# How far ahead of the first row stores a fused attention and routing kernel loads: three steps instead of seven, with four row buffers

## The chip, the core and the metric

The kernel runs on one core of one Trainium2 chip. The metric is the device time of one execution in microseconds (us). The core has a matrix engine (PE in the profile, with its weight loads as PEld), a vector engine (DVE), a scalar engine (ACT), a general engine (POOL) and a sync engine (SP), which here only issues DMAs; SPq is its queue in the trace. PEclk is the clock that the matrix engine was granted, as a share of full speed.

## What is computed

The reference runs a linear attention with decay over q, k and v of shape (4, 8, 768, 64), reshapes its result to 3072 rows of 512, and sends each row through one of eight feed-forward experts, chosen by the largest gate logit:

```python
for b in range(nb):                                   # blocks of 64 positions
    intra = einsum('bhic,bhjc->bhij', qb, kb) * Dmask
    intra = einsum('bhij,bhjd->bhid', intra, vb)
    inter = einsum('bhid,bhde->bhie', qb * lam_pow, kv_state)
    out[:, :, sl] = intra + inter
    kv_state = lam_block * kv_state + einsum('bhsd,bhse->bhde', kb * rev_pow, vb)
x = out.transpose(0, 2, 1, 3).reshape(B * S, H * D)   # 3072 x 512
logits = x @ w_gate
expert_idx = argmax(logits, axis=1)                   # and gate_w, its softmax weight
for e in range(8):
    out[mask] = gate_w[mask, None] * (maximum(xe @ w1[e], 0.0) @ w2[e])
```

All is in float32.

## The kernel before

**Two parts.** The first part, up to about 187 us of the trace, is the attention. It uses blocks of 128 positions, so there are six of them, and takes two of the four batches at a time: twelve steps, 0 to 11, in the order (block 0, batches 0 and 1), (block 0, batches 2 and 3), (block 1, batches 0 and 1) and so on. Every step leaves two row tiles x of 128 x 512, which are stored to a table `xs` in device memory. The second part gathers the rows of each expert from that table and runs the eight feed-forward passes. The lists that say which row goes to which expert (`slots`) are filled by POOL during the attention, by indirect DMAs (`put`, L422).

**One step, as the matrix engine runs it.** The loop at L832 overlaps three steps. In its turn i the engine first multiplies the attention output of step i-1 by a permutation with the gate's columns beside it (`leave`, then `rows`, L345 and L347, PSUM tiles `tx`), then transposes q and k of step i+1 (`turn_q` L234, `turn_k` L249), then does step i itself: q against the running state (L291), the state's growth `cp` (L320), scores against v (L303), q against the state once more (L291); and at the end the scores q k of step i+1 (L267). I call one turn of this loop a step. ACT copies each `tx` out of PSUM: the logits at L351, the row tile x at L353. DVE adds the grown state at L337, for which POOL has scaled the old one (L335). PE, DVE, ACT and SP run in exactly the order in which the code issues their work (`manual_schedule`, L114 and L823). An instruction that waits holds up everything behind it on its engine.

**Loads.** `load(i)` (L94) fetches q, k and v of a step with three DMAs of 512 KB, all on the SP queue (for step 0 they are halves, and k goes by the ACT queue). At L114 the loads of steps 0 to 6 are issued, before anything else on SP. From turn 3 on, each turn issues one more load, that of step i+4 (L835); it comes right behind the row stores of that turn. Loads 0, 1, 7 and 2, 3, 8 use buffers of the expert weights (`IN_WEIGHTS`), and the others use a pool of three.

**Row stores.** `store_rows` (L357) stores the two row tiles of step i-1 in turn i, with two DMAs of 256 KB on the SP queue. The row tiles rotate through three buffers (L341, tag `x`), so the copy at L353 into a fourth tile waits until the store of the first has landed. The feed-forward passes use the same tag for rows that they read back (L700).

**What else stands near.** `zeros` is a tile of 128 x 128 with a place of its own. DVE reads it once, in turn 0, for the decay tables (L773), and POOL stores a row of it to `xs` at the beginning (L780). In turn 8 the weights of the first pass are loaded (L837, 4 MB), in turn 10 the list of that pass, `list_0a` (L840, L458), and in turn 11 its rows are gathered and brought into blocks (`xg`, `xe`, `xb`). PE's first feed-forward products are L533.

Of the kernel before, what the change touches and what calls it, by code (L numbers as in the profile page):

```python
# [10 lines left out]
F32 = mybir.dt.float32  # L11
# [10 lines left out]
def kernel(  # L22
# [29 lines left out]
    nc = tc.nc  # L52
    B, H, S, D = q.shape
    N, MD = out.shape
    E = moe_w_gate.shape[1]
    F = moe_w1.shape[2]
    P = 128
# [19 lines left out]
    const = ctx.enter_context(tc.tile_pool(name="const", bufs=1))  # L77
# [10 lines left out]
    order = [(n, b) for n in range(NSTEP) for b in range(0, B, 2)]  # L88
    loaded = {}
    IN_WEIGHTS = {0: "w1", 1: "w1", 2: "w2", 3: "w2", 7: "w1", 8: "w2"}  # L90
    AT_ONCE = 7
    lam_bc = const.tile([P, H], F32, name="lam_bc")

    def load(i):  # L94

        n, b0 = order[i]
        shp = [P, 2, H, D]
        if i in IN_WEIGHTS:
            whole = wpool.tile([P, 3] + shp[1:], F32, tag=IN_WEIGHTS[i], name="qkv_in")
            loaded[i] = [whole[:, j] for j in range(3)]  # L100
        else:
            loaded[i] = [qkv.tile(shp, F32, tag=name, name=f"{name}_in") for name in "qkv"]
        per = 2 if i else 1
        for t, src in zip(loaded[i], (q, k, v)):
            queue = nc.scalar if i == 0 and src is k else nc.sync
            for b in range(0, 2, per):
                queue.dma_start(
                    out=t[:, b:b + per].rearrange("p b h d -> p (b h) d"),
                    in_=src[b0 + b:b0 + b + per, :, n * C:(n + 1) * C, :].rearrange(
                        "b h s d -> s (b h) d"))  # L110
            if i == 0 and src is q:
                nc.sync.dma_start(out=lam_bc, in_=lam.partition_broadcast(P))

    with tc.manual_schedule(engines={mybir.EngineType.SP}):  # L114
        for i in range(AT_ONCE):
            load(i)
# [16 lines left out]
    make_upper_triangular(nc, before, val=1.0, diag=False)  # L133
    ones = const.tile([P, P], BF16, name="ones")
    nc.vector.memset(ones, 1.0)
    zeros = const.tile([P, P], F32, name="zeros")
    nc.vector.memset(zeros, 0.0)

    rev = const.tile([P, E], F32, name="rev")
    nc.gpsimd.iota(rev, pattern=[[-1, E]], base=E, channel_multiplier=0,  # L140
# [56 lines left out]
    def load_weights(e, pin=lambda inst: inst):  # L197
        return load_first(e, pin), load_second(e, pin)
# [4 lines left out]
    work = ctx.enter_context(tc.tile_pool(name="work", bufs=2))  # L203
# [5 lines left out]
    def bank(i, shape, name):  # L209
        return ps.tile(shape, F32, tag=f"bank{i}", name=name)  # L210


    st = once.tile([P, B, HP, D], F32, tag="h2", name="st")
    halves = [slice(0, D), slice(D, P)]

    def pin(inst):
        return tc.keep_in_program_order(inst)
# [9 lines left out]
    def turn_q(m, s):  # L229
        shp = turned_shape  # L230
        tq = bank(2 * s, shp, "tq")
        for i, b in itertools.product(range(HP // 2), range(2)):
            h = s * HP + 2 * i
            nc.tensor.transpose(tq[:, i, b, :], m.q[:, b, h:h + 2, :], ident)  # L234
        qT = work.tile(shp, F32, tag="qT", name="qT")
        nc.scalar.copy(qT, tq)
        m.qT.append(qT)
        if m.n > 0:
            qsT = work.tile(shp, F32, tag="qsT", name="qsT", bufs=4)
            nc.vector.tensor_mul(  # L240
                qsT, tq, qdec[:, s * HP // 2:(s + 1) * HP // 2].unsqueeze(2).to_broadcast(shp))
            m.qsT.append(qsT)

    def turn_k(m, s):
        shp = turned_shape
        tk = bank(2 * s + 1, shp, "tk")
        for i, b in itertools.product(range(HP // 2), range(2)):
            h = s * HP + 2 * i
            nc.tensor.transpose(tk[:, i, b, :], m.k[:, b, h:h + 2, :], ident)  # L249
        kT = work.tile(shp, F32, tag="kT", name="kT")  # L250
        nc.scalar.copy(kT, tk)
        m.kT.append(kT)
        if m.n < NSTEP - 1:
            shp = [P, 2, HP, D]
            kd = work.tile(shp, F32, tag="kd", name="kd")
            hs = slice(s * HP, (s + 1) * HP)
            pin(nc.gpsimd.tensor_tensor(out=kd, in0=m.k[:, :, hs],  # L257
                                        in1=kdec[:, hs].unsqueeze(1).unsqueeze(3).to_broadcast(shp),
                                        op=ALU.mult))
            m.kd.append(kd)  # L260
# [77 lines left out]

    def rows(m, b, lg):

        x = work.tile([P, MD], F32, tag="x", name="x", bufs=3)  # L341
        tx = [bank(4 + 2 * b + c, [P, 2, W], f"tx{c}") for c in range(DC // 2)]
        for c, t in enumerate(tx):
            flat = t.rearrange("p j w -> p (j w)")
            nc.tensor.matmul(flat[:, :W], lhsT=m.xT[b][:, 2 * c, :], rhs=back[:, c, :W],  # L345
                                 start=True, stop=False, skip_group_check=True)
            nc.tensor.matmul(flat[:, P:P + W], lhsT=m.xT[b][:, 2 * c + 1, :],  # L347
                                 rhs=back[:, c, W:], start=False, stop=True,
                                 skip_group_check=True)
        for c, t in enumerate(tx):  # L350
            nc.scalar.copy(lg[:, c, :], t[:, 0, P:])  # L351

            nc.scalar.copy(x.rearrange("p (a d f) -> p d a f", a=P // Q, d=DC)[:, 2 * c:2 * c + 2],  # L353
                           t[:, :, :P].rearrange("p d (a f) -> p d a f", f=Q))
        m.x.append(x)
# [101 lines left out]
    def load_list(m):  # L457
        nc.sync.dma_start(out=m.list[:, :len(m.takes), :], in_=m.rows)  # L458
# [238 lines left out]
    def take_rows(m, ts):  # L697
        for t in ts:
            w = m.widths[t]
            m.y.append(work.tile([P, MD], F32, tag="x", name="y", bufs=3))  # L700
            pin(nc.sync.dma_start(out=m.y[t][:w], in_=m.ye[Q + t * P:Q + t * P + w, :]))

    def give_rows(m):
# [85 lines left out]
    def begin(i):  # L789
        n, b = order[i]  # L790
        m = SimpleNamespace(n=n, b=b, qT=[], qsT=[], kT=[], kd=[], mt=[], xT=[], x=[])
        m.q, m.k, m.v = loaded[i]
        return m
# [3 lines left out]
    def leave(m):  # L797
        for b in range(2):
            n, bs = group_of[m.n, m.b + b]
            i = bs.index(m.b + b)  # L800
            if i == 0:
                lgs[0] = small.tile([P, len(bs), DC // 2, E], F32, tag="lg", name="lg")
            rows(m, b, lgs[0][:, i])
        store_rows(m)
        if i == len(bs) - 1:
            chosen.append(choose(n, bs, lgs[0]))
            return chosen[-1]
# [15 lines left out]
    with tc.manual_schedule(engines={mybir.EngineType.PE, mybir.EngineType.DVE,  # L823
                                     mybir.EngineType.Activation, mybir.EngineType.SP}):
        cur, last = begin(0), None
        for s in range(2):
            turn_q(cur, s)
        for s in range(2):
            turn_k(cur, s)
        for s in range(2):  # L830
            score(cur, s)
        for i in range(len(order)):  # L832
            due = chosen.pop() if chosen else None
            new = leave(last) if last else None
            if i >= 3 and i + 4 < len(order):  # L835
                load(i + 4)
            if i == len(order) - 4:  # L837
                weights.append(load_weights(0))
            if i == len(order) - 2:
                load_list(passes[0])  # L840
            if i == len(order) - 1:
                for t in range(TE):
                    keep(passes[0], t)
                take_blocks(passes[0])
            ahead = begin(i + 1) if i + 1 < len(order) else None
            if ahead:
                for s in range(2):
                    turn_q(ahead, s)
                    turn_k(ahead, s)
            if i == 0:  # L850
                later_decays()
            if new:
                weigh(*new)
            if due:
                put(*due)
                if due[:2] == early:
                    start_early()
            attend_states(cur, 0)
            grow(cur)
            attend(cur)  # L860
            attend_states(cur, 1)
            to_sbuf(cur)
            update(cur)
            if i == len(order) - 2:
                for t in range(TE):
                    take(passes[0], t, 1 + (NSTEP - 2) * B * C)
            if ahead:
                for s in range(2):
                    score(ahead, s)
            last, cur = cur, ahead  # L870
        put(*chosen.pop())
        turn(passes[0])
        weigh(*leave(last))
        put(*chosen.pop())
# [95 lines left out]
    with tc.If(most > 0):  # L970
        for i in range(E):
            tiles = nc.values_load(beyond[0:1, i:i + 1], min_val=0, max_val=MORE)
            with tc.If(tiles > 0):
# [4 lines left out]
                with tc.For_i(0, tiles, 1) as r:  # L978
                    m = sized(P, 1)
# [36 lines left out]
```

## Time and profile before

| what | value |
|---|---|
| median of three timed runs | 511.45 us (508.19, 511.45, 511.73) |
| the profiled execution's own time | 507.75 us |
| its span, first to last instruction | 506.0 us |
| around the span | 1.75 us |
| PE busy | 438.6 us (87%) |
| DVE, POOL, ACT busy | 255.9, 253.8, 121.8 us |
| mean granted PE clock | 0.939 |
| DMA | 96.77 MB, mean 191 GB/s |

The profile's lines are read as follows. A group or a wait names the engine, the operation, the tiles as output<-input, and the line of the kernel as L341. A row of the timeline gives the start and the length in us, and in brackets how long the engine was idle before it and what ended that wait. A row of the stretches ("from:to length, ...") gives each engine's busy time with its instruction count, then PEclk, the busy share of the DMA engines (above 1 where packets overlap) and GB/s. A row of the waits gives the total, how many times, and the longest.

### The profile page before, as it was taken

The numbers are of one execution on the slowest core, as the hardware profiler recorded it, in microseconds if no ns is written. First come the engines' busy times: TensorE is split into PE (matmuls) and PEld (weight loads), VectorE is DVE, ScalarE is ACT, GpSimd is POOL, SyncE is SP. The second block draws the span as 40 slices with busy tenths as digits, with TensorE's granted clock in tenths as the row PEclk, the third lists the DMA queues.
The fourth block names the chain that finished last, engine by engine and source line by source line (L and its number), as shares of the span: only waits on it lengthen the run. The fifth ranks groups of instructions, "written<-read, shape, count | busy, mean of one in ns | idle before, by whom it ended". The sixth has DMA issues, their size and how long they took to land.

```text
span 506.0 us, 9177 instructions
## 1 busy us (share of the span) xinstructions
PE 438.6 (87%) x3559; PEld 409.1 (81%) x3559; DVE 255.9 (51%) x519; ACT 121.8 (24%) x300; POOL 253.8 (50%) x194
## 2 busy tenths in 40 slices
PE   4870596969698929999999999999999889999994
PEld 4760586959597718489999999999999889999963
DVE  3530245445255623105795592983593883594431
ACT  2420243424253310010310230231230120230410
POOL 6210232432523333268987559938279946279201
PEclk9995597979799969999999999999999989999998
DMA  9999574949592431896988967784989492963301
GB/s 180 237 221 218 141 156 98 200 95 197 116 339 81 148 84 28 241 341 198 290 276 215 367 196 243 206 278 116 307 277 263 124 316 98 281 215 82 119 18 48
DMA packets 131763, 96.77 MB, mean 191 GB/s; under 512 B 83600, under 2 KB 107412, under 8 KB 131711
## 3 DMA queue, kind: packets, MB, share of 16 engines
q1 hardware_dynamic: 124287, 82.16, 60.2%
q0 software_dynamic: 5344, 13.41, 8.8%
q10 hardware_dynamic: 2080, 0.52, 0.6%
q8 instruction: 30, 0.49, 0.4%
q14 instruction: 22, 0.18, 0.1%
HBM read 70.96 MB, written 25.20 MB: 190 GB/s over the span
## 4 chain that ended last, share of the span: by engine, by line
PE 48%; DVE 5%; SPq 3%; issue 3%; DMA 2%; POOL 1%; POOLq 0%; DVEq 0%
PE p L658 22%; PE p L634 22%; PE p L722 2%; DMA xb<-xe 1%; PE po L750 1%; DVE hT L618 1%; SPq L458 1%; SPq L481 1%; DMA xg<-xs,list 1%; SPq L495 1%; DVE yb L691 1%; DVE s_h L616 1%; DVE s_h L617 1%; DVE hT L642 0%; DVE xgT L525 0%
## 5 line engine op out<-in xcount | busy, mean ns | idle before, releaser
L504 POOL DMA_INDIRECT out_dram<-o,list x24 | 24.4, 1018 | 60.8 <-ACT o L710 39.5
L643 ACT ACTIVATE hT<-hT 128x408 f32<-128x408 f32 (+4 forms) x56 | 29.4, 527 | 100.9 <-DVE hT L642 96.7
L658 PE MATMUL p<-hT,w2t 128*128 128x204 f32 (+3 forms) x288 | 50.9, 330 | 0.0
L422 POOL DMA_INDIRECT slots<-entry,slot_i x24 | 23.5, 977 | 50.4 <-DVE slot_i L420 29.4
L658 PEld LDWEIGHTS p<-hT,w2t 128*128 128x128 f32 x288 | 48.3, 190 | 0.0
L634 PE MATMUL p<-xgT,w1t 128*128 128x204 f32 (+4 forms) x224 | 41.7, 328 | 0.7 <-DVE t_sd L564 0.7
L257 POOL TENSOR_TENSOR kd<-qkv_in,kdec 128x512 f32<-128x512 f32 x12 | 12.3, 1041 | 52.2 <-PE cp L320 40.4
L634 PEld LDWEIGHTS p<-xgT,w1t 128*128 128x128 f32 x224 | 37.4, 190 | 1.0 <-issue 1.0
L345 PE MATMUL tx<-back,xT 128*128 128x136 f32 x96 | 23.5, 332 | 15.4 <-DVE st L337 14.7
L273 DVE TENSOR_TENSOR mt<-sp,decay 128x512 f32<-128x512 f32 x48 | 29.9, 682 | 7.9 <-PE sp L267 7.5
L291 PE MATMUL op<-qsT,st 64*64 64x128 f32 x320 | 14.5, 290 | 21.7 <-ACT x L353 21.6
L642 DVE TENSOR_TENSOR hT<-p,u_qsT 128x408 f32<-128x408 f32 (+4 forms) x42 | 23.5, 559 | 17.7 <-PE p L634 16.5
L533 PE MATMUL ph<-xgT,w1t 128*128 128x256 f32 (+1 forms) x128 | 24.1, 350 | 8.9 <-DVE lg_sum L366 8.9
L345 PEld LDWEIGHTS tx<-back,xT 128*128 128x128 f32 x96 | 17.5, 225 | 17.0 <-issue 14.9
L574 POOL TENSOR_TENSOR s_k<-w1t 128x1024 f32<-128x1024 f32 x7 | 16.6, 2365 | 28.3 <-DMA w1t<-in_moe_w_dram 28.2
L533 PEld LDWEIGHTS ph<-xgT,w1t 128*128 128x128 f32 x128 | 20.7, 201 | 11.7 <-DVE lg_sum L366 9.1
L291 PEld LDWEIGHTS op<-qsT,st 64*64 64x64 f32 x320 | 9.3, 136 | 24.8 <-ACT x L353 22.2
L525 DVE STREAM_TRANSPOSE xgT<-xb 128x768 f32<-128x768 f32 (+3 forms) x16 | 16.5, 1029 | 25.2 <-DMA xb<-xe 24.8
L498 POOL DMA_INDIRECT xg<-xs,list x24 | 24.1, 1002 | 8.9 <-issue 5.4
L545 ACT COPY u_qT<-p 128x408 f32<-128x408 f32 (+5 forms) x21 | 10.0, 476 | 74.0 <-PE p L634 45.5
L267 PE MATMUL sp<-qT,kT 64*128 64x128 f32 x384 | 26.2, 280 | 1.1 <-issue 0.9
L337 DVE TENSOR_TENSOR st<-cp,sd 128x512 f32<-128x512 f32 x8 | 5.5, 692 | 42.1 <-POOL sd L335 33.4
(182 smaller groups left out, 1043.5 us busy)
## 6 DMA issues: line engine op xcount, KB each, us to landing
w1t<-in_moe_w_dram SPq DMA_DIRECT2D x8, 2048.0 KB
w2t<-in_moe_w_dram SPq DMA_DIRECT2D x8, 2048.0 KB
xs<-x SPq DMA_DIRECT2D x24, 256.0 KB
xe<-xg SPq DMA_DIRECT2D x21, 256.0 KB
y<-ye SPq DMA_DIRECT2D x17, 256.0 KB
q_in<-in_q_dram SPq DMA_DIRECT2D x6, 512.0 KB
k_in<-in_k_dram SPq DMA_DIRECT2D x6, 512.0 KB
v_in<-in_v_dram SPq DMA_DIRECT2D x6, 512.0 KB
```

The lines of the kernel that those rows point to most:

```text
L267: nc.tensor.matmul(sp[u][:, i, b, :], lhsT=m.kT[s][halves[u], i, b, :], rhs=m.qT[s][halves[u], i, b, :], start=(i == 0 and b == 0), stop=( ...
L273: nc.vector.tensor_mul(mt[:, u], sp[u], decay[:, u, s * HP // 2:(s + 1) * HP // 2].unsqueeze(2).to_broadcast(shp))
L291: nc.tensor.matmul(out_at(m, b, u, hp), lhsT=st[halves[u], m.b + b, hp, :], rhs=m.qsT[hp // 2][halves[u], hp % 2, b, :], start=(way == 0 a ...
L345: nc.tensor.matmul(flat[:, :W], lhsT=m.xT[b][:, 2 * c, :], rhs=back[:, c, :W], start=True, stop=False, skip_group_check=True)
L422: put = pin(nc.gpsimd.indirect_dma_start(out=slots, out_offset=bass.IndirectOffsetOnAxis(ap=slot_i[:, i:i + 1], axis=0), in_=entry[:, n, b ...
L498: return nc.gpsimd.indirect_dma_start(out=dst, out_offset=None, in_=xs[:rows, :], in_offset=bass.IndirectOffsetOnAxis(ap=idx, axis=0))
L504: put = nc.gpsimd.indirect_dma_start(out=out, out_offset=bass.IndirectOffsetOnAxis(ap=idx, axis=0), in_=src, in_offset=None, bounds_check= ...
L533: nc.tensor.matmul(ph, lhsT=w1t[:, dc, fc * P:(fc + 1) * P], rhs=m.xgT[:, dc, :, :m.h], start=(dc == 0), stop=(dc == DC - 1))
L634: nc.tensor.matmul(p[:, i, :], lhsT=lhs[:, dc, (c + i) * P:(c + i + 1) * P], rhs=rhs[:, dc, :], start=(dc == 0), stop=(dc == DH - 1))
L642: nc.vector.tensor_add(outs[i][k], p, u)
L643: nc.scalar.activation(outs[i][k], outs[i][k], ACT.Relu)
L658: nc.tensor.matmul(p[:, i, :], lhsT=rhs[:, fc, i * P:(i + 1) * P], rhs=lhs[:, fc, :], start=(fc == 0), stop=(fc == FC // 2 - 1))
```

## The change

`AT_ONCE` goes from 7 to 3, so loads 0, 1 and 2 stand ahead of the loop. Turn i then issues the stores of step i-1 and behind them load i+3. Turn 0 has no stores, so load 3 follows load 2 directly. The tag `x` gets four buffers in place of three, and `zeros` becomes the first tile of that tag, so its place is given to a row tile later.

```diff
-    AT_ONCE = 7
+    AT_ONCE = 3
...
-    zeros = const.tile([P, P], F32, name="zeros")
-    nc.vector.memset(zeros, 0.0)
...
     st = once.tile([P, B, HP, D], F32, tag="h2", name="st")
+    zeros = work.tile([P, P], F32, tag="x", name="zeros", bufs=4)
+    nc.vector.memset(zeros, 0.0)
...
-        x = work.tile([P, MD], F32, tag="x", name="x", bufs=3)
+        x = work.tile([P, MD], F32, tag="x", name="x", bufs=4)
...
-            m.y.append(work.tile([P, MD], F32, tag="x", name="y", bufs=3))
+            m.y.append(work.tile([P, MD], F32, tag="x", name="y", bufs=4))
...
-            if i >= 3 and i + 4 < len(order):
-                load(i + 4)
+            if i + AT_ONCE < len(order):
+                load(i + AT_ONCE)
```

What moves is the SP queue, at two places. The first is the beginning. Before, behind load 4 there stood the loads of steps 5 and 6 and then the row stores of steps 0, 1 and 2 (`q_in`, `k_in`, `v_in` and `qkv_in` are the buffers that a load fills, the number is the buffer's):

```order
L107 DMA q_in_97<-in_q_dram 128x16x64
L107 DMA k_in_98<-in_k_dram 128x16x64
L107 DMA v_in_99<-in_v_dram 128x16x64
L107 DMA q_in_103<-in_q_dram 128x16x64
L107 DMA k_in_104<-in_k_dram 128x16x64
L107 DMA v_in_105<-in_v_dram 128x16x64
L360 DMA xs_63<-x_362 128x512
L360 DMA xs_63<-x_373 128x512
L360 DMA xs_63<-x_488 128x512
L360 DMA xs_63<-x_499 128x512
L360 DMA xs_63<-x_658 128x512
L360 DMA xs_63<-x_669 128x512
```

Now, from load 3 (buffer 234) on, the same queue reads:

```order
L107 DMA qkv_in_234<-in_q_dram 128x16x64
L107 DMA qkv_in_234<-in_k_dram 128x16x64
L107 DMA qkv_in_234<-in_v_dram 128x16x64
L360 DMA xs_63<-x_344 128x512
L360 DMA xs_63<-x_355 128x512
L107 DMA q_in_368<-in_q_dram 128x16x64
L107 DMA k_in_369<-in_k_dram 128x16x64
L107 DMA v_in_370<-in_v_dram 128x16x64
L360 DMA xs_63<-x_476 128x512
L360 DMA xs_63<-x_487 128x512
```

The stores of step 0 have moved ahead of nine load DMAs, those of loads 4, 5 and 6, and the loads now stand between the stores, one step's load behind one step's stores.

The second place is the end of the attention, where the weights of the first feed-forward pass are loaded in turn 8. Before, the last load of q, k and v, that of step 11, stood one turn ahead of them:

```order
L107 DMA q_in_1360<-in_q_dram 128x16x64
L107 DMA k_in_1361<-in_k_dram 128x16x64
L107 DMA v_in_1362<-in_v_dram 128x16x64
L360 DMA xs_63<-x_1501 128x512
L360 DMA xs_63<-x_1512 128x512
L189 DMA w1t_1544<-in_moe_w1_dram 128x4x1024
L194 DMA w2t_1546<-in_moe_w2_dram 128x8x512
L360 DMA xs_63<-x_1676 128x512
```

Now it stands between the stores of turn 8 and the weights:

```order
L360 DMA xs_63<-x_1495 128x512
L360 DMA xs_63<-x_1506 128x512
L107 DMA q_in_1538<-in_q_dram 128x16x64
L107 DMA k_in_1539<-in_k_dram 128x16x64
L107 DMA v_in_1540<-in_v_dram 128x16x64
L187 DMA w1t_1544<-in_moe_w1_dram 128x4x1024
L192 DMA w2t_1546<-in_moe_w2_dram 128x8x512
L360 DMA xs_63<-x_1676 128x512
```

Every load of a middle step has moved one turn later, so that the last of them, 1.5 MB, is now issued directly ahead of the 4 MB of weights.

## The prediction

> **What bounds the kernel now.** I read the busy shares in slices first, then the waits, then the timeline around the hole that the slices show. On the page each digit is a slice of 12.65 us:
>
> ```profile
> PE   4870596969698929999999999999999889999994
> PEclk9995597979799969999999999999999989999998
> DMA  9999574949592431896988967784989492963301
> ```
>
> The reader is to see the fourth digit of PE: 0, while DMA is at 9. After about 230 us PE is nearly always at 8 or 9. So the second part is bound by PE, and time is to be had in the first. From the waits of 20 to 60 us:
>
> ```profile
> ACT x L353 <- DMA xs<-x: 23.2, 1, 23.2
> PE op L291 <- ACT x L353: 21.6, 1, 21.6
> ```
>
> PE waited once, 21.6 us, for a copy of ACT, and that copy waited for the landing of a row store. The timeline shows why the store was late:
>
> ```profile
> 24.06 0.38 ACT L353 COPY x<-tx 128x256 f32<-128x256 f32 x1
> 26.24 2.29 SPq L107 DMA_DIRECT2D qkv_in<-in_v_dram  x1
> 33.85 0.60 PE L249 MATMUL tk<-ident,qkv_in 128*128 128x128 f32 x4
> 47.80 2.35 SPq L107 DMA_DIRECT2D v_in<-in_v_dram  x1
> 50.26 6.42 SPq L360 DMA_DIRECT2D xs<-x  x4
> 55.61 0.37 ACT L353 COPY x<-tx 128x256 f32<-128x256 f32 x1 [23.16 <-DMA xs<-x]
> 56.04 1.47 PE L291 MATMUL op<-qsT,st 64*64 64x128 f32 x16 [21.58 <-ACT x L353]
> ```
>
> The row tiles of step 0 were ready at 24.06 + 0.38 = 24.44 us. SP issued their stores at 50.26, behind the last load DMA of step 6 (47.80). Three buffers hold both tiles of step 0 and one of step 1; the second tile of step 1 needs the first one's place, and gets it at 55.6. PE had gone on to the transposes for step 3 (33.85) and stood until 56.04. The wait that ends last here is a place in SP's queue.
>
> **The change, part by part.** *The stall that goes.* The stores of step 0 now stand behind load 3, whose last DMA is the row at 26.24. SP is free at 28.5, the tiles have been ready for 4 us, and the stores are issued at once. In the row above a store issued at 50.26 was landed when ACT started at 55.61, 5.3 us later, with load 6 still moving. The same delay gives 28.5 + 5.3 = 33.8 for the first store. With a fourth buffer nobody asks for it before step 3. The gap of 21.58 us goes whole, by both edits: ACT wanted the place at 55.61 - 23.16 = 32.45, so the earlier stores alone would leave 33.8 - 32.45 = 1.4 us, and the fourth buffer takes these.
>
> The fourth place is that of `zeros`, so its readers have to be done by 32 us:
>
> ```profile
> 7.57 0.59 POOL L780 DMA_DIRECT2D xs<-zeros  x1
> 14.63 1.37 DVE L773 TENSOR_TENSOR_SCAN qdec<-lam_pair,zeros 128x128 f32<-128x128 f32 x4
> xs<-zeros POOLq DMA_DIRECT2D x1, 2.0 KB, 5.4
> ```
>
> The scans end at 16.0, the small store lands at 7.57 + 5.4 = 13.0. The place is free 16 us early; a loss here is bounded by the 1.4 us above.
>
> *The clock that the stall cost.* After the gap PE ran slowly. The same work, from the first product with the state (L291) to the first scores (L267), in step 2 and in step 3:
>
> ```profile
> 62.98 2.06 PE L267 MATMUL sp<-qT,kT 64*128 64x128 f32 x32
> 68.80 0.67 PE L291 MATMUL op<-qsT,st 64*64 64x128 f32 x16
> 72.83 2.06 PE L267 MATMUL sp<-qT,kT 64*128 64x128 f32 x32
> 30.60:34.50 3.90, 3.85 (x34) 3.61 (x32) 1.68 (x3) 1.05 (x5) 0.00 (x0) 1.00 1.08 215
> 56.00:65.00 9.00, 8.96 (x129) 8.11 (x129) 5.04 (x19) 3.48 (x10) 3.03 (x3) 0.67 0.10 34
> 65.00:79.80 14.80, 9.92 (x165) 9.20 (x163) 4.56 (x11) 4.96 (x15) 7.11 (x7) 0.97 0.70 145
> ```
>
> In step 2 it took 62.98 - 56.04 = 6.94 us at a granted clock of 0.67, in step 3 it took 72.83 - 68.80 = 4.03 us at 0.97. Ahead of the gap, from 30.6 to 34.5, the clock was at 1.00, so without it 6.94 - 4.03 = 2.91 us go too. Together 24.49 us. By this step 3 begins at 64.96 - 24.49 = 40.5 us (its row is below).
>
> *What may take its place: loads that come late.* Loads from 4 on now stand behind stores. Sizes and pace:
>
> ```profile
> xs<-x SPq DMA_DIRECT2D x24, 256.0 KB
> q_in<-in_q_dram SPq DMA_DIRECT2D x6, 512.0 KB
> 7.68 2.50 SPq L107 DMA_DIRECT2D qkv_in<-in_k_dram  x1
> 15.60 0.63 PE L249 MATMUL tk<-ident,qkv_in 128*128 128x128 f32 x4 [1.59 <-DMA qkv_in<-in_k_dram]
> 30.59 0.50 PE L345 MATMUL tx<-back,xT 128*128 128x136 f32 x2
> 32.98 0.60 PE L249 MATMUL tk<-ident,qkv_in 128*128 128x128 f32 x4
> 34.50:56.00 21.50, 0.00 (x0) 0.00 (x0) 0.00 (x0) 0.39 (x3) 0.00 (x0) 0.58 1.25 232
> ```
>
> From 26.24 to 47.80 SP issued nine DMAs of 512 KB, one in 2.40 us, while the engines moved 232 GB/s: the queue runs at the pace of the DMA engines. A store is half as large; I take 1.2 us. So the stores of step 0 go at 28.5 and 29.7, and load 4 at 30.9 (q), 33.3 (k) and 35.7 (v). From issue to use it took between the store's 5.3 us and the 7.9 us of load 1's k (7.68 to 15.60, where PE waited for it). Then k of step 4 is there between 38.6 and 41.2 us. PE wants it at step 3's start plus what step 2 shows (its k at 32.98, 2.4 us behind the first `tx` of the step at 30.59), at 42.9. The margin is 1.7 to 4.3 us. I take no stall; the bound, if stores cost as much as a load's DMA, is 2 x 1.2 = 2.4 us later, 41.2 + 2.4 - 42.9 = 0.7 us. Load 3 is issued as before. For load 5 the stores of step 1 go at 38.1, its k at 42.9, there by 50.8, against 40.5 + 14.8 + 2.4 = 57.7: 7 us of margin. After that the demand is small:
>
> ```profile
> 64.96 0.50 PE L345 MATMUL tx<-back,xT 128*128 128x136 f32 x2
> 79.76 0.79 PE L345 MATMUL tx<-back,xT 128*128 128x136 f32 x2 [4.88 <-DVE st L337]
> 79.80:92.50 12.70, 12.70 (x161) 11.90 (x161) 7.31 (x23) 5.24 (x16) 3.03 (x3) 0.76 0.70 156
> ```
>
> Steps take 14.8 and 12.7 us in turn. A step moves 3 x 512 KB and 2 x 256 KB, 2.10 MB, which at 219 GB/s (512 KB in 2.40 us) is 9.6 us. The wait of 4.88 us for the state is paid again each second step whatever the loads do: POOL scales the state behind the indirect stores of the lists. It stays, and so does the slower clock behind it. [...]
>
> *The end of the attention.* The load of step 11 now goes directly ahead of the weights, which start some 3 x 2.4 = 7 us later against the steps.
>
> ```profile
> 139.40 0.43 SPq L189 DMA_DIRECT2D w1t<-in_moe_w_dram  x1
> 139.00:153.00 14.00, 14.00 (x232) 12.98 (x232) 8.72 (x28) 7.38 (x21) 3.03 (x3) 0.95 0.94 341
> 187.03 1.22 PE L533 MATMUL ph<-xgT,w1t 128*128 128x256 f32 x2 [8.91 <-DVE lg_sum L366]
> DMA to landing us min/median/max: 6.1/6.7/6.9
> ```
>
> They moved at 341 GB/s, so the 4.2 MB were there by about 153 and are not used before 187: 34 us of cover for 7. What that first product really waits for is the chain of list, gather and blocks, whose stores to the lists (last row) landed in 6.1 to 6.9 us in all 24 cases, with and without loads beside them. The weights now overlap the last ones. From zero to 2 us; I take 0.5, nearer the rows.
>
> *The second part.* Its row tiles get a fourth buffer too. It has no PE time to give:
>
> ```profile
> 234.00:506.00 272.00, 261.10 (x1520) 254.12 (x1520) 169.48 (x255) 55.70 (x104) 171.74 (x96) 0.99 0.67 207
> ```
>
> ```profile
> SPq L701 <- ACT o L710: 24.4, 3, 9.3
> ```
>
> PE is busy for 261 of 272 us. SP waits there 24.4 us in all for a place of such a tile (in SP's own waits), and a fourth can end that, but what SP brings there reaches a PE that is busy already. I take nothing, with a gain of up to 1.5 us out of PE's 10.9 idle ones as the lower bound; the part moves forward as a whole.
>
> **The sum.** 21.58 + 2.91 - 0 - 0.5 = 24.0 us. The profiled execution took 507.75 us by itself, which gives 483.8. The three timed runs (508.19, 511.45, 511.73) lie above it; the mean of the four is 509.8, and I forecast 509.8 - 24.0 = **485.8 us**.
>
> **The rivals.**
>
> *Loads late at two steps.* If loads 4 and 5 both come 3 us past PE's need, PE idles 3 us twice, and if that is enough for the slow clock it pays 2.91 us each time: 11.8 us back, 497.6 us. For it: the margin of load 4 is small, and a store may cost more than its bytes. Against it: load 5 has 7 us, and the engines kept up 215 to 232 GB/s in the stretches above.
>
> *The other side: the loads rule every step.* SP issues in order, so load i+3 waits for the copy of step i-1, and the loads lose the lead of four steps that they had. If loads and stores mixed move at less than some rate, each step lasts as long as its 2.10 MB. The last step's first row product:
>
> ```profile
> 169.10 0.50 PE L345 MATMUL tx<-back,xT 128*128 128x136 f32 x2
> ```
>
> From step 2 (30.59) to step 11 (169.10) the kernel took 138.5 us with the stall, nine steps at 15.4 us. So it decides from 2.10 MB / 15.4 us = 136 GB/s down. At 130 GB/s a step takes 16.1 us, nine take 145, 6.7 more than with the stall, and the time is 509.8 + 6.7 = 516.5 us. For it: the stretches from 65 to 92.5 us show 145 and 156 GB/s where loads and stores mix. Against it: the DMA engines are busy at 0.70 there, against 1.25 at 232 GB/s, so there was too little asked of them. [...]
>
> *It does nothing.* Should the place of `zeros` stay held, and the stores still land behind several loads, PE stands until a store of step 0 lands and the time stays at 509.8. The queue's order speaks against it: three loads fewer stand ahead.
>
> *The gain is lost at the hand-over* to the second part, with lists and weights in each other's way for 6 us: 492.
>
> **How the numbers follow.** The forecast holds with 0.80, late loads with 0.08, the hand-over with 0.06, the loads ruling with 0.03, nothing with 0.03. The forecast alone spans 507.75 - 24.5 - 1.5 = 481.8 (the second part's bound) to 511.73 - 24.5 + 0.7 + 2 = 489.9 (a late load 4, the full price at the end of the attention). To leave out no more than 2 in 10 I take in the hand-over and part of the late loads: 481.5 to 494. About 1% is what a measurement of this kernel can tell from no change. Faster by more: 0.80 + 0.08 + 0.06 = 0.94; within: 0.03; slower: 0.03.
>
> **What would show it.** Right: the wait of ACT at L353 for a store is gone, PE has no idle slice, step 3 begins near 40.5 us at full clock, its transposes wait for no load, and the first feed-forward product (187.03 before) starts near 163. Late loads would show as waits of PE at L234 or L249 for a DMA at steps 3 and 4. The prediction is wrong if step 3 begins after 45 us, or if the first feed-forward product moves by much less than step 3 does.

## The result, and the profile after

| what | before | after |
|---|---|---|
| median of four runs | 509.96 us (508.19, 511.45, 511.73, 508.47) | 485.63 us (483.61, 487.07, 487.94, 484.19) |
| the profiled execution, its span | 507.75, 506.0 us | 483.61, 481.8 us |
| mean granted PE clock | 0.939 | 0.964 |

The kernel is faster, by a ratio of 0.9524 [0.9457, 0.9591]. The forecast was 485.8 us; the saving is 24.3 us between the medians and 24.2 us between the spans, against a forecast of 24.0. Of experiment 6's five executions one ran at a mean granted clock of 0.56 and took 748.85 us, and its ratio is of the two fastest alone. The same row of the page as before, for PE, a slice now being 12.05 us:

```profile
PE   3899596969796499999899999999999799999994
```

PE has no empty slice any more. Of the holes of the first part two are left, a 4 at the 14th slice (156.6 to 168.6 us, the hand-over to the second part) and the weak slices at every second step. The timeline of the queue and of PE at the beginning:

```profile
28.90 2.82 SPq L360 DMA_DIRECT2D xs<-x  x2
...
32.26 2.86 SPq L107 DMA_DIRECT2D k_in<-in_k_dram  x1
32.30 0.38 ACT L353 COPY x<-tx 128x256 f32<-128x256 f32 x1
...
40.35 0.50 PE L345 MATMUL tx<-back,xT 128*128 128x136 f32 x2
...
42.75 0.60 PE L249 MATMUL tk<-ident,k_in 128*128 128x128 f32 x4
...
55.15 0.79 PE L345 MATMUL tx<-back,xT 128*128 128x136 f32 x2 [4.88 <-DVE st L337]
```

The first store goes at 28.90 (50.26 before). The copy that had waited 23.16 us for it (32.30, no bracket) waits for nothing, and step 3 begins at 40.35. k of step 4, issued at 32.26, is used at 42.75 without a wait. At 55.15 the wait of 4.88 us for the state stands as before. The stretches of steps 2 and 4 (length, PE, PEld, DVE, ACT, POOL, PEclk, DMA share, GB/s):

```profile
30.50:40.40 9.90, 9.90 (x164) 9.05 (x161) 6.96 (x22) 5.03 (x16) 3.04 (x3) 1.00 1.04 239
...
55.20:66.50 11.30, 11.30 (x161) 10.49 (x161) 7.47 (x23) 5.03 (x16) 3.03 (x3) 0.86 1.00 149
```

In step 2 loads and stores mix at 239 GB/s, more than the old gap had shown with hardly anything but loads (232), and PE is busy for all of 9.90 us at full clock. In step 4, the one behind that wait, the clock is 0.86 where it was 0.76; experiment 7 comes back to this.

**Where the 24.2 us of the span came from.** Both executions are divided at the same instructions: the first `tx` of steps 3, 9 and of the last row products behind step 11, and the first feed-forward product. The rows of before that have not been shown, and then those of after:

```profile
147.20 0.50 PE L345 MATMUL tx<-back,xT 128*128 128x136 f32 x2
...
164.31 0.39 SPq L458 DMA_DIRECT2D list_0a<-slots  x1
...
176.00 0.50 PE L345 MATMUL tx<-back,xT 128*128 128x136 f32 x2 [0.71 <-ACT xT L312]
```

```profile
120.10 0.50 PE L345 MATMUL tx<-back,xT 128*128 128x136 f32 x2
...
132.87 0.47 PE L345 MATMUL tx<-back,xT 128*128 128x136 f32 x2 [2.85 <-DVE st L337]
...
139.95 0.38 SPq L458 DMA_DIRECT2D list_0a<-slots  x1
...
150.38 0.50 PE L345 MATMUL tx<-back,xT 128*128 128x136 f32 x2 [0.60 <-ACT xT L312]
...
163.66 1.22 PE L533 MATMUL ph<-xgT,w1t 128*128 128x256 f32 x2 [11.16 <-DVE lg_sum L366]
```

| stretch | before | after | gain |
|---|---|---|---|
| start to step 3 | 64.96 | 40.35 | 24.61 |
| step 3 to step 9 | 82.24 | 79.75 | 2.49 |
| step 9 to the last row products | 28.80 | 30.28 | -1.48 |
| to the first feed-forward product | 11.03 | 13.28 | -2.25 |
| second part | 318.97 | 318.14 | 0.83 |
| sum | 506.0 | 481.8 | 24.20 |

The first stretch came as computed (24.49). The forecast of the total is as near as it is because four other amounts, two gains and two losses of some 1 to 2.5 us, nearly cancel. The experiments are on the cause of the first and on the smaller ones in the attention; none is on the second part.

### The profile page after: what moved, and what is told of

It is laid out like the page before. It is cut to its first block, busy times and chain, and to the rows that moved or that the text cites. A ratio compares the mean times of both kernels' runs of the same rounds, so it can differ in the third digit from the quotient of the medians.

```text
span 481.8 us, 9168 instructions
## 1 busy us (share of the span) xinstructions
PE 431.1 (89%) x3559; PEld 402.9 (84%) x3559; DVE 257.4 (53%) x519; ACT 121.5 (25%) x300; POOL 253.2 (53%) x194
## 4 chain that ended last, share of the span: by engine, by line
PE 45%; DMA 6%; DVE 5%; POOL 4%; issue 3%; SPq 2%; POOLq 0%
PE p L658 23%; PE p L634 19%; DMA xe<-xg 3%; PE p L722 3%; DMA xg<-xs,list 2%; POOL xg L498 2%; PE po L750 1%; DVE s_h L617 1%; DVE hT L618 1%; SPq L458 1%; DVE yb L691 1%; DVE s_h L616 1%; DVE hT L642 0%; POOL t_q L574 0%; POOL w2t L574 0%
## 5 line engine op out<-in xcount | busy, mean ns | idle before, releaser
L642 DVE TENSOR_TENSOR hT<-p,u_qsT 128x408 f32<-128x408 f32 (+4 forms) x42 | 23.5, 559 | 17.1 <-PE p L634 16.9
L498 POOL DMA_INDIRECT xg<-xs,list x24 | 24.3, 1014 | 8.9 <-issue 5.1
L665 DVE TENSOR_TENSOR yT<-p,u_qsT 128x408 f32<-128x408 f32 (+3 forms) x18 | 10.2, 568 | 27.2 <-PE p L658 27.1
L267 PE MATMUL sp<-qT,kT 64*128 64x128 f32 x384 | 24.7, 279 | 0.1
L267 PEld LDWEIGHTS sp<-qT,kT 64*128 64x128 f32 x384 | 22.4, 188 | 2.2 <-issue 1.9
```

The lines of the kernel that those rows point to most:

```text
L267: nc.tensor.matmul(sp[u][:, i, b, :], lhsT=m.kT[s][halves[u], i, b, :], rhs=m.qT[s][halves[u], i, b, :], start=(i == 0 and b == 0), stop=( ...
L498: return nc.gpsimd.indirect_dma_start(out=dst, out_offset=None, in_=xs[:rows, :], in_offset=bass.IndirectOffsetOnAxis(ap=idx, axis=0))
L642: nc.vector.tensor_add(outs[i][k], p, u)
```

## The experiments

My theory: the stall came from the place of the first row stores in SP's queue, behind loads that nobody needed yet, and is as long as those loads hold the store. The rivals: that the fourth buffer is what counts; and that a shorter lead of the loads costs something which the gain hides.

**1. The fourth buffer alone, with seven loads ahead.**

```diff
 # on the kernel before
-    zeros = const.tile([P, P], F32, name="zeros")
...
+    zeros = work.tile([P, P], F32, tag="x", name="zeros", bufs=4)
...
-        x = work.tile([P, MD], F32, tag="x", name="x", bufs=3)
+        x = work.tile([P, MD], F32, tag="x", name="x", bufs=4)
...
-            m.y.append(work.tile([P, MD], F32, tag="x", name="y", bufs=3))
+            m.y.append(work.tile([P, MD], F32, tag="x", name="y", bufs=4))
```

> Seven loads ahead as before, but four buffers for the row tiles with zeros as the first tile of the tag: the buffer half of the change alone. Theory (the stall is the place of the first stores behind the loads on SP; the buffers only decide which tile meets it): SP still issues the first store near 50.3 us and it lands near 55.6. With four places the tiles of steps 0 and 1 all find one, and the first tile of step 2 is the one that waits, from about 41.2 us. Step 3 begins at 40.4 as in the changed kernel, ACT waits some 14 us for a store, PE stands from about 44.2 to 56 (12 us) and pays the slow clock (2.9 us) again. Against before that is 9.5 us less: about 500.5 us. Rival (one more buffer is what counts): no wait for a store, about 486 us. Rival (only the order counts): no gain, 510 us.

It took 497.77 us (496.56 to 498.90), ratio 0.9758 [0.9715, 0.9801]: neither the time of after nor that of before, and 2.7 us less than the 500.5 expected.

```profile
51.40 2.28 SPq L360 DMA_DIRECT2D xs<-x  x1
...
56.71 0.37 ACT L353 COPY x<-tx 128x256 f32<-128x256 f32 x1 [15.54 <-DMA xs<-x]
...
57.48 0.19 PE L409 MATMUL rank<-oh,before 128*128 128x32 bf16 x1 [13.37 <-ACT x L353]
```

The store goes at the old time (51.40) and ACT still waits for it until 56.71, but it is a tile of step 2 that waits and no longer one of step 1: PE gets through step 2 first (step 3 begins at 40.24) and then stands 13.37 us instead of 21.58 (some 12 were expected). A buffer more moves the wait by one tile; it doesn't take it away.

**2. Three loads ahead, with three buffers.** The edit is the reverse of the one above, on the kernel after.

> Three loads ahead with stores and loads in turn, but three buffers for the row tiles and zeros in a place of its own: the order half of the change alone. Theory: the first store is issued near 28.9 us, lands 5.3 us later at 34.2, and the second tile of step 1 wants its place at 32.45, so ACT waits 1.4 to 1.8 us once and PE as long or less, with no slow clock behind it; 487 us. A further wait is possible at step 10, where the stores of step 8 stand behind the weights with one step less of slack: up to 4 us more, 491. Rival (order alone does nothing, the buffer is the cure): 500 us or more.

It took 486.85 us (483.75 to 490.04), ratio 0.9548 [0.9508, 0.9588], which the runs can't tell from after's 0.9524. The profile can:

```profile
34.48 0.37 ACT L353 COPY x<-tx 128x256 f32<-128x256 f32 x1 [2.14 <-DMA xs<-x]
...
34.91 1.00 PE L291 MATMUL op<-qsT,st 64*64 64x128 f32 x16 [0.56 <-ACT x L353]
...
41.61 0.50 PE L345 MATMUL tx<-back,xT 128*128 128x136 f32 x2
...
143.10 1.45 PE L291 MATMUL op<-qsT,st 64*64 64x128 f32 x16 [1.71 <-ACT x L353]
```

ACT waits 2.14 us for the first store (the prediction had 1.4), PE only 0.56 of that, and step 3 begins 1.26 us later than with four buffers. The further wait that was thought possible came too: ACT's longest wait for a row store was 4.3 us, for a store that was held behind the weights (SP issued them at 120.55, the stores at 124.82), PE lost 1.71 us by it, and step 10 took 14.57 us against 10.79 in after. So in the new order the fourth buffer is worth 1.3 us at the beginning and 3.8 in step 10; the shorter hand-over behind it (10.20 us against 13.28) gave most of the second amount back, and the medians lie 1.2 us apart. The order does nearly all.

**3. Five loads ahead, four buffers.** A dose between three and seven: `AT_ONCE = 5` on the kernel after.

> The changed kernel with AT_ONCE = 5: loads 0 to 5 stand ahead of the first stores, four buffers. Theory (each load ahead of the stores delays them by 7 us, and the stall begins when the first store lands after the first tile of step 2 wants its place at 41.2 us): the first store is issued near 43 and lands near 48.5, ACT waits some 7 us in step 3, PE stands about 5.5 and pays the slow clock of 2.9 us: 492 to 495 us. Rival (any turn-by-turn order is good enough): 485.6 us. Rival (the four steps of lead before were worth something): below 485.6 us.

It took 490.51 us (489.44 to 492.58), ratio 0.965 [0.9594, 0.9706].

```profile
43.10 2.88 SPq L360 DMA_DIRECT2D xs<-x  x1
...
48.70 0.37 ACT L353 COPY x<-tx 128x256 f32<-128x256 f32 x1 [7.48 <-DMA xs<-x]
...
49.46 0.18 PE L409 MATMUL rank<-oh,before 128*128 128x32 bf16 x1 [5.31 <-ACT x L353]
...
61.67 0.57 PE L345 MATMUL tx<-back,xT 128*128 128x136 f32 x1 [4.17 <-DVE st L337]
```

The waits of ACT and PE are as expected (7 and 5.5), and the time is 1.5 us under the lower end, because the stall cost less behind it: step 4 begins at 61.67 against 55.15, 6.5 us later, of which 5.31 are the stall, so the slow clock added only 1.2 us net (the first products with the state behind the stall took 1.47 us at 49.81, the next ones 0.67 at 54.84). Part of the reason is in the last row: the next wait for the state became 4.17 in place of 4.88. (In experiment 1 the same step began 14.56 us later than in after, 1.19 more than the stall, with a wait of 3.06 for the state.) With the earlier rows the dose is complete. From the issue of the first store to the copy that waited for it took 5.35 us before, 5.31 in experiment 1, 4.80 in experiment 2 (from 29.68) and 5.60 here; ACT's wait is that landing less the time at which it wanted the place, 23.16, 15.54, 2.14 and 7.48 us, and none in after.

**4. Two loads ahead.** `AT_ONCE = 2` on the kernel after.

> The changed kernel with AT_ONCE = 2: one step less of lead, load i+2 in turn i, four buffers. Theory (the loads have few us of margin): load 3 now stands behind the stores of step 0, its k goes near 29.3 us and is there at 34.6 to 37.2 against a wish at 32.9, so PE waits 1.7 to 4.3 us in step 2; in the short steps of 11 to 12 us a load has 13.7 us from the tiles to the wish for k and needs 12.8 to 15.4, so up to 2 us more in each of four: 488 to 495 us, with the waits at L234 and L249 for a DMA. Rival (the lead is not used at all beyond one step): 485.6 us. Rival (the loads then rule every step): over 505 us.

It took 492.14 us (490.97 to 496.66), ratio 0.9681 [0.9626, 0.9736], inside the range expected, but not for the reason given.

```profile
25.25 2.27 SPq L107 DMA_DIRECT2D qkv_in<-in_k_dram  x1
...
33.09 0.60 PE L249 MATMUL tk<-ident,qkv_in 128*128 128x128 f32 x4
...
117.78 3.49 SPq L187 DMA_DIRECT2D w1t<-in_moe_w_dram  x1
...
126.84 12.96 SPq L107 DMA_DIRECT2D k_in<-in_k_dram  x1
...
141.84 1.09 PE L234 MATMUL tq<-ident,q_in 128*128 128x128 f32 x4 [5.00 <-DMA q_in<-in_q_dram]
```

I expected PE to wait for k of load 3 in step 2. It doesn't: SP issued it at 25.25, not at 29.3 as I had worked out, and 7.84 us later it was used without a wait (33.09). Up to step 9 the steps begin within 0.7 us of after's. The time goes in turn 10: the last load now stands behind the 4 MB of weights (117.78), SP needs 12.96 us to hand over its k, and PE waits 5.00 us for q and then 1.34 for k, 6.3 in all; with the slow clock behind them (the transposes of q and k took 1.06 to 1.09 us there, against 0.60 at 33.09) step 10 took 8.3 us longer than in after. So a lead of two steps is enough here as long as no long transfer stands ahead of a load.

**5. Two loads ahead, and the weights behind the last load.** This was to test that reading: on experiment 4, `if i == len(order) - 4:` becomes `- 3`, so the weights are issued in turn 9 instead of 8.

> AT_ONCE = 2 with the weights of the first pass moved from turn 8 to turn 9, behind load 11. With the weights in turn 8, AT_ONCE = 2 took 492.1 us, and the profile showed PE waiting for loads only in turn 10, 5.0 and 1.3 us for load 11, which stood behind the weights; between steps 2 and 9 no load was late. Theory (two steps of lead are enough for the loads by themselves, and the loss was the place of load 11): no wait at L234 or L249 for a DMA, 484 to 487 us. Rival (the loads are late at the end because the lead is short): the wait in turn 10 stays above 3 us and the time above 489 us.

It took 494.32 us (492.00 to 497.13), ratio 0.9712 [0.9639, 0.9785], no gain where 5 to 8 us were expected.

```profile
33.20 0.63 PE L249 MATMUL tk<-ident,qkv_in 128*128 128x128 f32 x4 [0.17 <-DMA qkv_in<-in_k_dram]
...
171.84 0.79 PE L533 MATMUL ph<-xgT,w1t 128*128 128x256 f32 x1 [16.65 <-DVE lg_sum L366]
```

The reading of the waits was right and the forecast of the time wrong. From step 1 (21.57) to the end of the attention PE waits 0.17 us for a load (33.20), so two steps of lead do; but the first feed-forward product comes at 171.84, later than in experiment 4, after a wait of 16.65 us. The last row products had come 6.3 us earlier (153.07 against 159.36): the wait went on to the hand-over.

**6. The row stores on another queue.** On the kernel before, with seven loads ahead and three buffers, the stores are issued by ACT.

```diff
-            nc.sync.dma_start(out=xs[r0:r0 + C, :], in_=x)
+            nc.scalar.dma_start(out=xs[r0:r0 + C, :], in_=x)
```

> The kernel before with one word changed: the row stores are issued by ACT's queue in place of SP's; seven loads ahead, three buffers. Theory (the wait is the order of issue on SP, not the bytes in front): the stores are issued when the tiles are ready, near 24.5 us, go beside the loads and land by 30 to 33, so the stall of 21.6 us and the slow clock behind it (2.9) go, less what ACT loses by issuing (some 0.5 to 1 us in each step, up to 8 us): 486 to 494 us. Rival (the DMA engines are full to 55 us and a store lands only when the loads ahead of it are through): the wait of ACT for a store stays near 20 us and the time near 510 us.

Four executions took 496.36, 499.22, 505.86 and 503.89 us, all above the 486 to 494 expected; the first two give a ratio of 0.9766 [0.9709, 0.9823]. The profile below is that of a further execution.

> The kernel before with the row stores issued by ACT's queue, once more for a profile at full clock: the first one was taken at a granted clock of 0.56 throughout, and its four other executions took 496 to 506 us against an expected 486 to 494. Theory (the stall is gone and ACT's issuing costs more than I thought): no wait of ACT or PE for a store before 60 us, step 3 begins by 42 us, and the 10 us that are missing lie in later steps or behind them. Rival (stores still land late beside the loads): ACT waits for a store for 10 us or more between 32 and 55 us, and step 3 begins near 52 to 55 us.

It took 503.80 us (span 502.0). The timeline:

```profile
23.84 0.89 ACTq L360 DMA_DIRECT2D xs<-x  x2
...
40.44 0.50 PE L345 MATMUL tx<-back,xT 128*128 128x136 f32 x2
...
143.72 1.73 SPq L481 DMA_DIRECT2D xe<-xg  x2
...
155.11 1.13 PE L533 MATMUL ph<-xgT,w1t 128*128 128x256 f32 x4 [1.01 <-DVE lg_sum L366]
...
213.36 2.58 POOL L574 TENSOR_TENSOR t_v<-w2t,t_k 128x1024 f32<-128x1024 f32 x1
213.77 2.62 DVE L567 TENSOR_TENSOR t_kd<-xgT,t_xT 128x424 f32<-128x424 f32 x1
```

For the stall this is the cleanest run of all. The loads stand in SP's queue as before (the last DMA of step 6 at 50.74), the stores don't stand behind them (23.84), and step 3 begins at 40.44, with three buffers. So it is the order in one queue that made the wait, not the amount of data in flight. ACT's issuing of the two stores of step 0 took 0.89 us (23.84), within the 0.5 to 1 us a step that I had estimated. The attention ends even earlier than in after: first feed-forward product at 155.11, against 163.66. The time is lost in the second part, 346.9 us (155.11 to the span's end) against 318.1. One reason is in the rows at 213 us: a DVE sum that began within a sum of POOL over the weights took 2.62 us and ended 0.45 behind it. The same sum took 0.60 us in the kernel after, where POOL's next sum began at 211.57:

```profile
210.04 0.60 DVE L567 TENSOR_TENSOR t_kd<-xgT,t_xT 128x424 f32<-128x424 f32 x1
```

The seven sums of that line took 10.7 us in all (1.52 us in the mean, 2.57 again at 440.13), against 3.9 in after, where they took 0.53 to 0.60 each. That is 6.7 us of DVE's time, and other lines show the same (L566 took 2.73 us at 211.00, and 8.7 us in all against 3.9). Much of the rest is an early start that is not used: the first of these sums comes 58.7 us after the first feed-forward product here and 46.4 us after it in the kernel after. Why the sums of the two engines coincide in this version, why DVE's then take longer, and what makes up the 28.8 us, was not tested; this profile is of one of the longer executions, and in the shortest, with the same first part, some 21 us would remain (an estimate, 496.36 against 503.80).

**7. The weights earlier.** The two losses of the account (step 9 to the feed-forward product, 3.7 us) I put to the weights, which the change had brought nearer to the list. On the kernel after, `len(order) - 4` becomes `- 6`, so they are issued in turn 6.

> The changed kernel with the weights of the first feed-forward pass loaded in turn 6 in place of turn 8, behind load 9 and ahead of load 10. Theory (the 2.25 us that the change lost between the last row product and the first feed-forward product come from list stores that land late beside the weights, up to 11.9 us against 6.9): the list stores of turn 9 land in 6 to 7 us again, the list is read about 2.7 us sooner, the hand-over takes 11.0 us in place of 13.3, no transposes wait for load 10, and the time is 483.4 us. Rival (the list stores are late for another reason, or nothing waits for them): the hand-over stays at 13 us and the time at 485.6. Rival (loads behind 4 MB come late): waits at L234 in turn 8 or 9 and 488 us or more.

It took 485.10 us (480.03 to 485.82), ratio 0.9521 [0.9469, 0.9573]: no difference from after, and the theory fell.

```profile
55.02 0.79 PE L345 MATMUL tx<-back,xT 128*128 128x136 f32 x2 [4.89 <-DVE st L337]
...
67.67 0.50 PE L345 MATMUL tx<-back,xT 128*128 128x136 f32 x2
...
139.57 0.39 SPq L458 DMA_DIRECT2D list_0a<-slots  x1
...
145.85 0.50 PE L345 MATMUL tx<-back,xT 128*128 128x136 f32 x2
...
147.55 1.25 SPq L360 DMA_DIRECT2D xs<-x  x2
148.89 2.27 SPq L481 DMA_DIRECT2D xe<-xg  x2
```

Step 9 begins at 122.32 here, so the list is issued 17.25 us behind it, as before the change (164.31 - 147.20 = 17.11) and sooner than in after (139.95 - 120.10 = 19.85). That is of no use, for the rows gathered with it are written on (`xe`) at 148.89 by the same queue, behind the row stores of step 11's turn (147.55), 3.04 us after that step's first `tx` (145.85). The same distance shows in both main kernels, before and then after (step 11 of before begins at 169.10):

```profile
172.21 0.91 SPq L481 DMA_DIRECT2D xe<-xg  x2
176.72 1.81 SPq L495 DMA_DIRECT2D xb<-xe  x4
```

```profile
143.66 0.50 PE L345 MATMUL tx<-back,xT 128*128 128x136 f32 x2
...
146.70 1.21 SPq L481 DMA_DIRECT2D xe<-xg  x2
154.23 1.80 SPq L495 DMA_DIRECT2D xb<-xe  x4
```

172.21 - 169.10 = 3.11 us before, 146.70 - 143.66 = 3.04 in after. So the list doesn't set the pace there. What is longer in after is the next step, from `xe` to `xb`: 154.23 - 146.70 = 7.53 us against 4.51, and 5.79 here (`xb` at 154.68). Why that transfer took longer stays open. In experiment 6, where the row stores are on another queue, `xe` went at 143.72, ahead of step 11 (its first `tx` at 145.38).

The first two rows settle another amount of the account. Up to turn 6 this run issues the same work as after. Yet its step 4, behind the same wait, took 67.67 - 55.02 = 12.65 us, as before the change (12.74), and not the 11.33 of after. So the gain of 2.49 us between steps 3 and 9 is something in which executions of the same instructions differ, and it can't be credited to the change.

**8. The next bound: the lists behind the state.** The waits of 4.88 us for the state stayed, as predicted, because POOL scales the state behind the indirect stores of the lists. Here these stores are issued behind the scaling.

```diff
 # on the kernel after; put() ends before the indirect stores, drop() holds them
-                put(*due)
+                placed = put(*due)
...
             update(cur)
+            if due:
+                drop(*placed)
...
-        put(*chosen.pop())
+        drop(*put(*chosen.pop()))
```

> The changed kernel with the indirect list stores of a turn issued behind the scaling of the state on POOL, in place of ahead of it (one of four still goes ahead, as the scheduler has it). It tests whether the loads would rule if the steps were shorter, and what bounds the changed kernel. Theory (PE's wait of 4.8 us for the state in every second step, and the slow clock behind it, are all that stands between the steps of 14.8 and 11.3 to 12.3 us and one of about 10 us; the loads, 9.6 us a step by their bytes, keep up): the waits at L345 for the state fall to 1 us or less, steps take 10 to 11 us, and the time is 464 to 469 us. Rival (the loads rule as soon as a step nears 9.6 us): waits at L234 and L249 for loads, 470 to 478 us. Rival (the state's wait is not the list stores): 485.6 us.

It took **472.61 us** (472.35 to 473.88), ratio 0.9302 [0.9249, 0.9356], the fastest version of the study, and 3.6 us over the range that I expected.

```profile
51.44 0.47 PE L345 MATMUL tx<-back,xT 128*128 128x136 f32 x2 [1.08 <-DVE st L337]
...
109.87 2.83 SPq L187 DMA_DIRECT2D w1t<-in_moe_w_dram  x1
...
131.71 0.37 ACT L353 COPY x<-tx 128x256 f32<-128x256 f32 x1 [7.08 <-DMA xs<-x]
...
152.05 1.22 PE L536 MATMUL ph<-xgT,w1t 128*128 128x256 f32 x2 [10.47 <-DVE lg_sum L366]
```

```profile
51.40:61.20 9.80, 9.76 (x160) 9.01 (x160) 7.53 (x23) 5.03 (x16) 5.33 (x6) 1.00 0.86 143
```

The first fence is the timeline, the second the stretch of step 4. The wait is down to 1.08 us, the clock is whole, and steps 4 and 5 take 9.8 and 10.9 us, where 2.10 MB have to come and go in each. From step 1 on PE waits 0.20 us for a load in all (at 24.39), so the rival that loads rule every step is out with steps a third shorter than the 15.4 us that it was computed for. One thing that fell short of the expectation stands at 131.71: a stall of the old kind, 7.08 us of ACT and 6.66 of PE behind it, for a row tile whose place is held by a store behind the 4 MB of weights (109.87), this time with four buffers.

**9. The same, with the weights one turn later.** `len(order) - 3` on experiment 8.

> The kernel with the list stores behind the state's scaling, and the weights of the first feed-forward pass moved from turn 8 to turn 9, behind the row stores of step 8. With the short steps, ACT waited 7.1 us in turn 11 for the store of a row tile of step 8, issued behind the 4 MB of weights, and PE 6.7 us behind it. Theory (a store behind a long transfer in SP's queue holds its buffer, the same mechanism as the stall at the start): with the stores of step 8 ahead of the weights the wait in turn 11 goes, step 11 takes about 7 us in place of 15.8, the first feed-forward product starts 6 to 7 us earlier, near 145.5 us, and the time falls from 472.6 to 465 to 468 us. Rival (the gather of the first pass and its lists are the bound there whatever PE does): the wait goes, but the first feed-forward product stays near 152 us and the time near 472.

It took 474.41 us (470.27 to 475.69), ratio 0.9344 [0.9287, 0.94], not to be told from experiment 8. The rival was right.

```profile
132.44 1.00 POOL L501 DMA_INDIRECT xg<-xs,list_0a  x1 [19.20 <-DMA xs<-x]
...
150.04 1.22 PE L536 MATMUL ph<-xgT,w1t 128*128 128x256 f32 x2 [19.78 <-DVE lg_sum L366]
```

PE's stall is gone (ACT still waits 1.67 us for a store) and the last row products come at 128.14 instead of 139.46, but the first feed-forward product moves by only 2 us: POOL's gather begins at 132.44, and PE waits 19.78 us. The bracket names a row store, but the gather's own list went out only at 121.69, ahead of the last stores in the same queue; which of the two came last the run doesn't say.

## Why the prediction was right

- **The stall that goes (21.58 us) and the clock behind it (2.91).** Right as computed: step 3 begins at 40.35, forecast 40.5. Experiments 1, 3 and 6 show the cause, since the wait ends 4.8 to 5.6 us behind the issue of the first store (50.26, 51.40, 43.10 and, in experiment 2, 29.68), and goes when the store has a queue without loads. The share given to the fourth buffer (1.4 us) was measured at 1.26; that it also saves a second wait, in step 10 (experiment 2), the prediction didn't have.
- **Late loads, taken at nothing.** Right. The k of load 4 was there after at most 42.75 - 32.26 = 10.5 us, with no wait. The margins were wider than I thought: with even less lead, k of load 3 was used without a wait 7.84 us after its issue (experiment 4), and 0.17 us late after 8.12 (experiment 5). That is near the 7.9 us which I took as the upper bound.
- **The wait for the state stays, with its slow clock.** Half right. The 4.88 us stayed, the price of the clock behind them isn't fixed: steps 4, 6 and 8, which follow such a wait, were shorter by 1.41, 0.72 and 0.38 us in the profile after, 2.51 in all, at a granted clock of 0.86, 0.81 and 0.79 against 0.76, 0.77 and 0.77 before. That is the gain of 2.49 us between steps 3 and 9, which the forecast didn't have. It isn't the change's: in experiment 7 the same instructions paid the old price (step 4, 12.65 us). What sets the price of one such wait is not shown; I had taken it as fixed.
- **The end of the attention, 0.5 us (bound 2).** The term that was mis-sized: 3.73 us went between step 9 and the first feed-forward product. The reason given (lists beside weights) didn't hold. With the weights out of the way the list came early again and the time stayed (experiment 7). Of this loss 1.48 us lie ahead of the last row products. Step 9 took 12.77 us in both, but in after PE idled 2.85 us at its end and step 10 then ran at a granted clock of 0.84 for 10.79 us; before, PE issued its last products with small gaps, idled 0.31 us, and step 10 ran at 1.00 for 9.13. Experiments 1 to 7 all show a wait of 2.84 to 3.23 us there, experiment 6 with the loads and the buffers of before, so the short step 10 may belong to the one execution that was profiled before the change; no run settles it. The other 2.25 us lie behind it, where the transfer from `xe` to `xb` took 3.0 us more, for a cause that stays open.
- **The second part, nothing.** Right within 0.83 us; no run here separates that from the spread of the runs.
- **The rivals.** Late loads and loads that rule were refuted by rows of after and, at steps of 9.8 us, of experiment 8. That a load 3 us late costs 2.91 us of slow clock besides, the rival's term, no run shows; in experiment 4 PE waited 6.3 us for loads in a step that became 8.3 us longer. The hand-over that loses 6 us was the one that came nearest: it lost 2.25 here, and took back most or all of what the attention had gained in experiments 5 and 9.

So the time was right by its main term, and its nearness, 0.2 us, is luck of the small ones.

## What to carry to other kernels

In a queue that issues in order (SP's, where the first store went at 50.26 us behind seven loads, at 43.10 behind six and at 28.90 behind four), a store that frees a buffer must not stand behind loads that nobody needs yet: date both sides, and let the lead of the loads be what the use needs (here 8 us from issue to use, under one step) rather than what the buffers allow. A buffer more only moved the wait by one tile here (PE's 21.58 us became 13.37), while the order alone left 2 of 23 us of the first wait here. The same pattern returned at other places of that queue: weights ahead of a load (6.3 us of PE, experiment 4), weights ahead of a row store (6.66 us of PE, experiment 8), row stores ahead of the gathered rows (`xe` 3.04 us behind step 11's first `tx`, experiment 7). So after each gain look for the next thing that stands behind something it doesn't need.

## What the runs showed of the hardware

- The same wait of 4.88 us was followed by a step at a granted clock of 0.76 before and 0.86 after, 1.4 us apart, and two executions of the same instructions differed as much (step 4, 12.65 us in experiment 7 and 11.33 in after). A wait of 2.85 us was followed by a step at 0.84; with a wait of 1.08 us (experiment 8) the step ran at 1.00.
- A sum on DVE took 2.62 us where it began within one of POOL's sums over the weights (213.77, POOL's from 213.36 to 215.94, experiment 6), and 0.60 in after (210.04), ahead of POOL's next sum (211.57). An operation of L642 that began within another of POOL's sums (223.78, POOL's from 223.47 to 226.08, experiment 6) took 0.59. What makes the difference is not shown.
- A step that loads 1.5 MB and stores 0.5 MB moved 239 GB/s (30.5 to 40.4 us of after), against 232 in the old gap, so stores mixed among the loads took nothing from the rate there.
